# Moving the load of w4 behind two chunks of transposes, and the waits for the outputs to GpSimd

## The chip, the cores and the metric

The kernel runs on one core of a Trainium2 chip. The metric is the device time of one execution in microseconds; the time of a kernel is the median of its runs. A profile is one execution with the hardware profiler on. It gives times relative to the start of the program's span.

## What is computed

A gated mix of two blocks over one sequence of S = 2048 tokens with D = 640 channels, all in bf16. Block A is linear attention with 32 heads of 20; block B mixes tokens by shifts and ends in an MLP with F = 1728. Both read the same x.

```python
def reference(A_x, A_wqkv, A_wo, B_x, B_w1, B_w2, B_w3, B_w4, gate_w):
    ...                      # _A_ref: phi(q) (phi(k)^T v) / (phi(q) . sum phi(k)), then @ wo
    def _B_ref(x, w1, w2, w3, w4):
        h = _gelu(_layernorm(x, axis=-1) @ w1)
        ...                  # hs: four column groups of h, shifted by +1, -1, +2, -2 tokens
        hs = jnp.concatenate([g0, g1, g2, g3], axis=-1) @ w2
        x1 = x + hs
        h2 = _gelu(_layernorm(x1, axis=-1) @ w3) @ w4
        return x1 + h2
    x = A_x
    g = _sigmoid((x * gate_w).sum(-1, keepdims=True))
    a = _A_ref(x, A_wqkv, A_wo)
    b = _B_ref(x, B_w1, B_w2, B_w3, B_w4)
    return g * a + (1 - g) * b
```

## The kernel before

The tokens are cut into 16 tiles of 128 (t, u = 0 to 15) and four chunks of 512 (c = 0 to 3). The kernel works in stages that overlap: q and k for all tiles; the products of k with x, from which the attention's small matrix is made (item "kvt" multiplies it with the v weights, "lt", "m" and "mq" with wo; "ms" stores 40 rows of it to device memory and "mt" loads them back into M_sb); the first normalization (items "n1", "t1"), w1 with gelu, w2; the second normalization ("n2", "t2"), w3 with gelu into h2T, and w4. The attention tiles ("a") multiply the normalized q, transposed into pqnT (items "qs", "qn", "qt"), with M_sb. The last VectorE step of a tile (line 645) adds what w4 gave, and out_tiles stores the result from x_tok.

Engines: TensorE multiplies. ScalarE does exp, gelu and copies out of PSUM. VectorE does sums, scaling and residual adds. GpSimd normalizes (normalize writes one of four xn slots, line 628), computes the statistics, and scales x_tok into abx ahead of an attention tile. SyncE's queue issues nearly all DMAs: loads, stores and the transposes of xn into xnT (t_xn, four semaphores in turn, "trn0" to "trn3"), of pq_tok into pqnT (qt_tile) and of tlT into tl. The lines 285 and 289 of the helper dma are the transposes and the plain DMAs; line 318 is a wait that stands as an instruction of its own; line 321 is the closing barrier, and line 1404 holds the opening one.

The order of each engine's instructions is fixed when the kernel is built. Every step is an item of a stream with dependencies. The planner (_Items.run) keeps its own clock for every engine and issues, again and again, the item that could start first in that clock; items whose entry has duration 0 go ahead of matmul items, and among equals the longest remaining path decides. An item's dependencies count as done when its last instruction or DMA ends in the planner's clock. On the chip only the order in each engine's queue and the semaphores count: the helper _Sched keeps, for each address range, who wrote and read it, and adds the waits that are needed.

The loads of w3 and w4 are two items of the stream "MISC":

```python
    def w3_load():
        dma_in(w3[:, :, 0:F], B_w3.rearrange("(k p) f -> p k f", p=128), "w3")

    def w4_load():
        dma_in(w4[:, 0:KFF, :], B_w4[0:128 * KFF, :].rearrange("(k p) f -> p k f", p=128), "w4a")
        dma_in(w4[0:64, KFF, :], B_w4[128 * KFF:F, :], "w4b")
        dma_in(w4[64:128, KFF, :], B_w4[128 * KFF:F, :], "w4c")
```

KFF is 13: F is 13 blocks of 128 and one of 64, and the last 64 rows of w4 are loaded twice, for the groups that work with half of TensorE's rows (w3_half at line 1120, w4_enter at lines 1208 and 1213). The w4 tensor lies in memory that the first half of the kernel uses for wq, Er, wv and the first tiles of pk_tok. Items that depend on "w4load" are the attention tiles "a" (a planner's dependency only; they do not read w4) and the item of the second w3_half with the first w4_enter, which reads it.

At the end of the program, emit appends waits for the last DMA on each output semaphore, the last output first, and then the barrier. In the barrier each engine executes a DRAIN and reports; GpSimd collects the reports and releases all engines. The last tile's output leaves in two stores, 512 columns from ScalarE's queue and 128 from SyncE's.

Of the kernel before, what the change touches and what calls it, by code (L numbers as in the profile page):

```python
# [15 lines left out]
NT = S // 128  # L16
# [35 lines left out]
class _Sched:  # L52
# [247 lines left out]
    def emit(self):  # L300
        nc = self.nc
        with ExitStack() as es:
            sems = {}
            for e in ("pe", "act", "dve", "pool"):
                sems["c:" + e] = es.enter_context(nc.semaphore("cnt_" + e))
            for k in self.dma_cnt:
                sems["d:" + k] = es.enter_context(nc.semaphore("dma_" + k))
            seen = {w for p in self.prog.values() for (waits, _fn, _sem) in p for w in waits}
            last = {k: i for i, k in enumerate(self.out_order)}
            left = [k for k in self.dma_cnt if k not in last and ("d:" + k, 16 * self.dma_cnt[k]) not in seen]  # L310
            for k in sorted(last, key=last.get, reverse=True) + left:
                self.prog["sp"].append(([("d:" + k, 16 * self.dma_cnt[k])], None, None))
            engs = {"pe": nc.tensor, "act": nc.scalar, "dve": nc.vector, "pool": nc.gpsimd, "sp": nc.sync}

            for name, e in engs.items():
                for (waits, fn, sem) in self.prog[name]:
                    for (sk, val) in waits:
                        e.wait_ge(sems[sk], val)
                    if fn is not None:
                        fn(e).then_inc(sems[sem], 16 if sem.startswith("d:") else 1)  # L320
            nc.all_engine_barrier()
# [95 lines left out]
def _build(nc, A_x, A_wqkv, A_wo, B_w1, B_w2, B_w3, B_w4, gate_w, out, dbg=None, stop=None):  # L417
# [336 lines left out]
    IT = _Items()  # L754
# [521 lines left out]
    for c in range(NCH):  # L1276
        for j in range(KD):
            deps = [(("t1", u), 0.9) for u in range(4 * c, 4 * c + 4)] if j == 0 else []
# [6 lines left out]
    for t in range(NT):  # L1285
        c = t // 4
        deps = [(("w1", c, KD - 1), GEL)]
# [8 lines left out]
    for u in range(NT):  # L1296
        deps = [(("s2", u // 4), 3.2 + 0.9 * (u % 4))]
# [4 lines left out]
        IT.add("N2", ("n2", u), 0.0, lambda u=u: normalize(2, u, st2), deps)  # L1302
        IT.add("T2", ("t2", u), 0.0, lambda u=u: t_xn(2, u), deps=[(("n2", u), 1.1)])
    IT.add("MISC", ("w3load",), 0.0, w3_load, deps=[(("k", NT - 1), 0.0), (("t1", NT - 1), 0.0)])
    IT.add("MISC", ("w4load",), 0.0, w4_load, deps=[(("kvt",), 0.0), (("t1", NT - 1), 0.0), (("z", NT - 1), 1.5)])
    for c in range(NCH):
        for j in range(KFF):
            deps = []
# [4 lines left out]
            if j == 0:  # L1313
                deps = deps0 + [(("t2", u), 0.9) for u in range(4 * c, 4 * c + 4)]
# [11 lines left out]
    for t in range(NT):  # L1326
        deps = [(("zb",), 1.0), (("qr", max(t // 4, 1)), 2.0)]
# [14 lines left out]
    for t in range(NT):  # L1342
        c = t // 4
        deps = [(("qt", t), 3.0), (("w4load",), 0.0), (("mq",), 1.0), (("mt",), 2.5)]
# [38 lines left out]
def bass_gated_mix__linear_attn_block__mixer_s_mlp__prompt_kernel(  # L1383
    nc, A_x, A_wqkv, A_wo, B_x, B_w1, B_w2, B_w3, B_w4, gate_w, out
):
    assert tuple(A_x.shape) == (1, S, D) and tuple(out.shape) == (1, S, D)
    assert tuple(A_wqkv.shape) == (D, 3 * D) and tuple(A_wo.shape) == (D, D)
    assert tuple(B_w1.shape) == (D, D) and tuple(B_w2.shape) == (D, D)
    assert tuple(B_w3.shape) == (D, F) and tuple(B_w4.shape) == (F, D) and tuple(gate_w.shape) == (D,)
    _build(nc, A_x, A_wqkv, A_wo, B_w1, B_w2, B_w3, B_w4, gate_w, out)  # L1390
# [28 lines left out]
```

## Time and profile before

| | |
|---|---|
| median of 3 runs | 260.21 us (259.76 to 260.26) |
| profiled execution, its own time | 260.06 us |
| its span | 258.3 us, granted clock 1.00 |
| busy share of the span | TensorE 99%, VectorE 61%, ScalarE 43%, GpSimd 37% |
| DMA moved | 26.78 MB, mean 104 GB/s |

The profile's names: PE is TensorE's matmuls, PEld its weight loads, DVE is VectorE, ACT ScalarE, POOL GpSimd, SP SyncE; a q behind the name means the engine's sequencer, which waits, branches and issues DMAs. A row of groups names line, engine, operation, output<-inputs and count. In rows of one line or tile the three numbers after the count are the shortest, median and longest duration in ns, then come the first and last start in us. In rows of stretches each engine's busy time is followed by its number of instructions; the last three numbers are TensorE's granted clock, the mean busy share of the 16 DMA engines and the GB/s moved. The span does not hold all of the time: 260.06 - 258.3 = 1.76 us lie outside it.

### The profile page before, as it was taken

Reading aid. Unit: us, or ns where it says so; the run is one execution under the profiler, and the core shown is the slowest. Engines: PE = TensorE matmul, PEld = TensorE weight load, DVE = VectorE, ACT = ScalarE, POOL = GpSimd, SP = SyncE. Lnnn points to the kernel's source line nnn. Section 1 sums busy time; section 2 is a strip of 40 time slices with the busy share of each in tenths; the row PEclk is TensorE's granted clock in tenths of the full one; section 3 lists DMA queues with packets and bytes.
Section 4 is the critical chain, followed back from the end, with each engine's and each line's share of the span. In section 5 each row is a group of like instructions: output and inputs, shape, how many; then the busy total and the mean of one; then the engine's idle time right before and its main releaser. Section 6 shows DMA issues by size and latency. Waiting matters only on the chain.

```text
span 258.3 us, 3824 instructions
## 1 busy us (share of the span) xinstructions
PE 254.8 (99%) x1427; PEld 122.7 (47%) x1427; DVE 158.2 (61%) x293; ACT 110.9 (43%) x229; POOL 96.8 (37%) x154
## 2 busy tenths in 40 slices
PE   7999999999999999999999999999999999999996
PEld 3555555544444554554444444444444444444443
DVE  2597877899954699989995302999022530134076
ACT  1496777751355857684874240005500045200100
POOL 8014996869934119659681210111020120021000
DMA  6857997826527699483668512114200140000224
GB/s 194 263 101 235 139 141 193 231 55 119 102 49 105 124 392 305 82 101 65 127 124 117 102 20 23 25 25 130 42 3 0 20 124 0 0 0 1 43 84 139
DMA packets 58644, 26.78 MB, mean 104 GB/s; under 512 B 49966, under 2 KB 57215, under 8 KB 58626
## 3 DMA queue, kind: packets, MB, share of 16 engines
q1 hardware_dynamic: 57122, 22.92, 42.5%
q0 software_dynamic: 1168, 3.28, 5.4%
q10 hardware_dynamic: 336, 0.35, 0.4%
q8 instruction: 11, 0.18, 0.3%
q14 instruction: 7, 0.06, 0.1%
HBM read 12.09 MB, written 2.67 MB: 57 GB/s over the span
## 4 chain that ended last, share of the span: by engine, by line
PE 97%; DMA 1%; DVE 0%; issue 0%
PE ps L606 61%; PE ps L1233 22%; PE ps L812 7%; PE ps L893 2%; PE ps L792 1%; DMA x_tok<-in_A_x_dram 1%; PE ps L1120 1%; PE ps L1208 1%; PE ps L617 1%; PE ps L914 1%; PE ps L894 0%; PE ps L984 0%; PE ps L793 0%; PE ps L1213 0%; PE ps L1017 0%; DVE xT L671 0%
## 5 line engine op out<-in xcount | busy, mean ns | idle before, releaser
L606 PE MATMUL ps<-xnT,w 128*128 128x512 bf16 x360 | 81.3, 379 | 0.0
L606 PEld LDWEIGHTS ps<-xnT,w 128*128 128x128 bf16 x360 | 34.6, 98 | 39.3
L645 DVE SCALAR_TENSOR_TENSOR x_tok<-ps,stg,abx 128x512 bf16<-128x512 f32 (+2 forms) x17 | 12.2, 718 | 58.5 <-PE ps L1233 58.4
L1233 PE MATMUL ps<-w,h2T 128*128 128x512 bf16 (+2 forms) x221 | 47.2, 366 | 0.0
L628 POOL TENSOR_SCALAR abx<-x_tok,stg 128x512 f32<-128x512 bf16 x16 | 12.0, 753 | 88.2 <-DVE x_tok L645 70.1
L628 POOL TENSOR_SCALAR xn<-x_tok,st 128x640 bf16<-128x640 bf16 x32 | 38.6, 1215 | 8.6 <-DMA xnT<-xn 8.2
L662 ACT ACTIVATE h2T<-ps 128x512 bf16<-128x512 f32 x52 | 29.9, 599 | 22.7 <-PE ps L606 22.6
L1233 PEld LDWEIGHTS ps<-w,h2T 128*128 128x128 bf16 x221 | 21.2, 98 | 24.1
L662 ACT ACTIVATE tlT<-ps 128x512 bf16<-128x512 f32 x8 | 4.8, 597 | 64.1 <-PE ps L606 41.9
L662 ACT ACTIVATE Er<-ps 128x640 bf16<-128x640 f32 (+1 forms) x35 | 22.9, 658 | 17.8 <-PE ps L606 9.7
L661 ACT ACTIVATE junk<-x_tok 128x640 bf16<-128x640 bf16 x32 | 23.6, 737 | 4.7 <-DVE x_tok L643 4.2
L662 ACT ACTIVATE hsT<-ps 128x512 bf16<-128x512 f32 (+1 forms) x32 | 18.9, 593 | 14.2 <-PE ps L606 13.8
L606 PE MATMUL ps<-w,hsT 128*128 128x512 bf16 (+1 forms) x160 | 24.0, 299 | 0.0
L606 PE MATMUL ps<-wkg,xT 128*128 128x512 bf16 (+1 forms) x150 | 22.6, 299 | 0.0
L606 PE MATMUL ps<-M_sb,pqnT 128*128 128x512 bf16 x80 | 19.7, 379 | 0.0
L606 PEld LDWEIGHTS ps<-w,hsT 128*128 128x128 bf16 x160 | 13.4, 98 | 12.5
L645 DVE SCALAR_TENSOR_TENSOR abx<-ps,stg,abx 128x512 f32<-128x512 f32 x16 | 12.0, 750 | 10.7 <-PE ps L606 7.2
L606 PEld LDWEIGHTS ps<-wkg,xT 128*128 128x128 bf16 x150 | 12.6, 97 | 11.7
L643 DVE SCALAR_TENSOR_TENSOR x_tok<-ps,x_tok 128x640 bf16<-128x640 f32 x16 | 13.1, 821 | 7.6 <-PE ps L606 6.9
L812 PE MATMUL ps<-pk_tok,x_tok 128*128 128x512 bf16 x80 | 17.8, 379 | 0.0
L636 DVE TENSOR_TENSOR qprod<-qprod,pk_tok 128x640 f32<-128x640 f32 x13 | 16.3, 1252 | 0.5
L628 DVE TENSOR_SCALAR Er<-Er 128x640 bf16<-128x640 bf16 (+1 forms) x35 | 11.6, 332 | 7.6 <-ACT Er L662 6.8
(85 smaller groups left out, 282.9 us busy)
## 6 DMA issues: line engine op xcount, KB each, us to landing
w<-in_B_w_dram SPq DMA_DIRECT2D x1, 2160.0 KB, 9.5
w<-in_B_w_dram SPq DMA_DIRECT2D x1, 2080.0 KB, 15.0
x_tok<-in_A_x_dram SPq DMA_DIRECT2D x3, 640.0 KB, 5.6
out_dram<-x_tok SPq DMA_DIRECT2D x3, 640.0 KB, 3.5
w<-in_B_w_dram POOLq DMA_DIRECT2D x8, 160.0 KB, 6.2
wkg<-in_A_wqkv_dram SPq DMA_DIRECT2D x5, 160.0 KB, 3.9
wv<-in_A_wqkv_dram POOLq DMA_DIRECT2D x1, 800.0 KB, 5.6
x_tok<-in_A_x_dram SPq DMA_DIRECT2D x4, 160.0 KB, 3.2
```

What stands on the lines that cost most here:

```text
L606: ins = e.matmul(out_ap, l, r, start=(i == 0), stop=(i == n - 1))
L617: ins = e.transpose(o, s_, ident[:])
L628: return engf(lambda e: e.tensor_scalar(out_ap, in_ap, s1, s2, op0, op1), rd, [out_ap], cost=cost)
L636: return engf(lambda e: e.tensor_tensor(out_ap, a, b_, op), [a, b_], [out_ap], cost=cost)
L643: return dve(lambda e: e.scalar_tensor_tensor(out_ap, in0, scalar, in1, op0, op1, accum_out=accum), rd, [out_ap, accum], cost=cost + 70.0)
L645: return dve(lambda e: e.scalar_tensor_tensor(out_ap, in0, scalar, in1, op0, op1), rd, [out_ap], cost=cost)
L661: return act(lambda e: e.activation(out_ap, in_ap, func, bias=bias, scale=scale, accum_out=accum), rd, wr, cost=cost)
L662: return act(lambda e: e.activation(out_ap, in_ap, func, bias=bias, scale=scale), rd, wr, cost=cost)
L792: e.matmul(ps[:, b, :], l, x_tok[:, t, 0:512], start=(t == 0), stop=(t == NT - 1))
L812: ins = e.matmul(ps[:, b, :], l, r, start=(t0 + q_ == 0), stop=(t0 + q_ == NT - 1))
L893: e.matmul(ps[:, b, 0:512], l, w[:, k, 0:512], start=(k == 0), stop=(k == KD - 1))
L1233: ins = e.matmul(o, l, r, start=False, stop=(i == KFF - 1), skip_group_check=shared)
```

## The change

Two edits. The waits for the outputs, with those for DMAs that nothing else waited for, are appended to GpSimd's program instead of SyncE's. And the item "w4load" gets other dependencies: instead of the last tile of the first normalization's transposes ("t1", 15) and the last addition of z ("z", 15), it now depends on the store of the 40 rows ("ms") and on the eighth transpose of the second normalization ("t2", 7). The dependency on "kvt" stays. The item keeps its place in its stream, behind "w3load".

```diff
@@ -309,7 +309,7 @@
             for k in sorted(last, key=last.get, reverse=True) + left:
-                self.prog["sp"].append(([("d:" + k, 16 * self.dma_cnt[k])], None, None))
+                self.prog["pool"].append(([("d:" + k, 16 * self.dma_cnt[k])], None, None))
@@ -1302,7 +1302,7 @@
     IT.add("MISC", ("w3load",), 0.0, w3_load, deps=[(("k", NT - 1), 0.0), (("t1", NT - 1), 0.0)])
-    IT.add("MISC", ("w4load",), 0.0, w4_load, deps=[(("kvt",), 0.0), (("t1", NT - 1), 0.0), (("z", NT - 1), 1.5)])
+    IT.add("MISC", ("w4load",), 0.0, w4_load, deps=[(("kvt",), 0.0), (("ms",), 0.0), (("t2", 7), 0.0)])
```

## The prediction

> **What bounds the kernel now.** I read the page first: engine totals, then the chain that ended last in order of time.
>
> ```profile
> span 258.3 us, 3824 instructions
> ...
> PE 254.8 (99%) x1427; PEld 122.7 (47%) x1427; DVE 158.2 (61%) x293; ACT 110.9 (43%) x229; POOL 96.8 (37%) x154
> ```
>
> TensorE is busy for 254.8 of 258.3 us, and nearly every piece of the chain is its own. A busy share of 99% can still hide matmuls that start late, so I take pieces of the chain in order of time (start, length, what, how many).
>
> ```profile
> 127.91 22.77 PE ps L606 x105
> 150.68 2.28 PE ps L1120 x20
> ...
> 205.62 16.19 PE ps L606 x75
> ...
> 239.18 16.99 PE ps L1233 x91
> 256.17 0.03 issue
> 256.19 0.35 DVE x_tok L645
> ```
>
> Between 127.91 and 150.68 there are 105 matmuls at 22.77 / 105 = 0.217 us each; in a late stretch 75 of the same kind take 16.19 / 75 = 0.216 us each. The first stretch lies right behind the place to which the load is moved, and it is full without a gap: 105 x 0.001 us is all that could be won in it. The chain ends with TensorE at 256.17 and a last VectorE step at 256.19 to 256.54. What is left, 256.54 to 258.3, is the last store and the closing barrier. So the change has two places where it can act: the stretch from 88 to 151 us, by making TensorE wait, and the last 1.8 us.
>
> **The load of w4, where it goes away.** It now stands in SyncE's queue behind w3's load. Issues (size, microseconds to landing), then the same issues with their own durations (shortest/median/longest ns, first and last start), then stretches with TensorE's busy time ahead of the other engines', and at the end the DMA share and GB/s.
>
> ```profile
> w<-in_B_w_dram SPq DMA_DIRECT2D x1, 2160.0 KB, 9.5
> w<-in_B_w_dram SPq DMA_DIRECT2D x1, 2080.0 KB, 15.0
> ```
> ```profile
> L289 SPq DMA_DIRECT2D w<-in_B_w_dram x4: 523/936/5852, 88.1 to 95.2; - x4
> ```
> ```profile
> 88.00:95.00 7.00, 7.00 (x46) 3.60 (x44) 5.95 (x15) 4.26 (x9) 0.20 (x1) 1.00 0.92 304
> 95.00:100.00 5.00, 5.00 (x32) 2.59 (x31) 4.90 (x11) 4.61 (x11) 3.57 (x7) 1.00 1.05 370
> ...
> sum 63.00, PE 63.00 PEld 30.61 DVE 49.79 ACT 39.76 POOL 32.97; mean PE 3.94 PEld 1.91 DVE 3.11 ACT 2.48 POOL 2.06
> ```
>
> w3 and w4 together keep the DMA engines full (shares 0.92 and 1.05), and one of the four issues holds SyncE for 5.85 us. Yet the last row sums sixteen stretches from 88 to 151 us, and TensorE is busy in 63.00 of 63.00. Taking w4 out of 88 to 104 us makes transposes behind it land earlier, but nothing on the path was late: gain 0.
>
> **Where it goes to.** SyncE's queue there, by the timeline of its issues (start, time until the group's last issue ended):
>
> ```profile
> 100.80 13.82 SPq L285 DMA_TRANSPOSE xnT<-xn  x8
> 114.66 0.56 SPq L289 DMA_DIRECT2D m_rows<-Mt  x1
> 118.91 5.29 SPq L285 DMA_TRANSPOSE xnT<-xn  x4
> 124.30 8.26 SPq L285 DMA_TRANSPOSE pqnT<-pq_tok  x6
> 132.66 5.76 SPq L285 DMA_TRANSPOSE xnT<-xn  x4
> ```
>
> The first eight xnT transposes are the two chunks that the load is to follow; its other new dependency, the store of m_rows, stands at 114.66. So three issues (one of 2080 KB, two of 80 KB) move past eight transposes and one store, and come to stand at 115.22, in front of the ninth transpose. That one waits for GpSimd's xn until 118.91, so SyncE has 118.91 - 115.22 = 3.69 us free.
>
> Cost of the three issues: at best 3 x 0.52 = 1.6 us, which the 3.69 hide. At worst the stall of 5.85 comes along, with one issue of the shortest and one of the median length: 0.52 + 5.85 + 0.94 = 7.3 us, and the ninth transpose goes out 7.3 - 3.69 = 3.6 us late. I take the lower end, because the issue of 5.85 us stood behind w3's 2160 KB, which is no longer in front of it. The data is 2240 KB, 2.29 MB; at the 304 to 370 GB/s of the rows above that is 6.2 to 7.5 us, so it lands at about 123, and at the worst, with the old 15.0 us, at 131.
>
> Who waits for what stands behind it:
>
> ```profile
> L606 PE MATMUL ps<-M_sb,pqnT x80: 379/379/379, 138.6 to 234.2; 128*128 128x512 bf16 x80
> ```
> ```profile
> L1213 PE MATMUL ps<-h2h,w x8: 269/274/280, 152.9 to 238.9; 64*128 64x256 bf16 x8
> ```
> ```profile
> L285 SPq DMA_TRANSPOSE xnT<-xn x16: 1200/1276/1795, 100.8 to 136.6; - x16
> ...
> DMA to landing us min/median/max: 2.6/2.7/4.7
> ```
> ```profile
> 129.10 4.66 POOL L628 TENSOR_SCALAR xn<-x_tok,st 128x640 bf16<-128x640 bf16 x4
> ```
>
> w4 itself is first read at 152.9: at least 22 us after the latest landing. The first pqnT transpose goes out at 124.3 and lands 2.7 later, at 127.0; TensorE first reads pqnT at 138.6, a margin of 11.6. The last xnT transpose starts at 136.6 and, with the longest landing of 4.7, is there by 141.3; it is read by the half-width groups at 150.68, a margin of 9.4. GpSimd's xn slots of the fourth chunk wait for the third chunk's transposes; the first of those lands at 118.91 + 2.7 = 121.6 and GpSimd starts at 129.10, a margin of 7.5. Even the worst delay, 3.6 us of queue and a landing longer by 4.7 - 2.6 = 2.1, is 5.7 and under all of these. The cover is TensorE's queue of w3 groups (the 105 matmuls); without it each microsecond of delay would be one of time. In the planner the attention tiles wait for the load too; the first of them, the reader of pqnT at 138.6, comes after the latest landing of 131, so TensorE's order has no reason to change. Moved load: 0.
>
> **The waits at the end.** The last store, SyncE's waits for the outputs, and the closing barrier (L321), beside the opening barrier (L1404) and GpSimd's last work:
>
> ```profile
> L289 SPq DMA_DIRECT2D out_dram<-x_tok x1: 345/345/345, 256.6 to 256.6; - x1
> ...
> DMA to landing us min/median/max: 1.5/1.5/1.5
> ```
> ```profile
> L318 SPq EVENT_SEMAPHORE  x2: 137/457/777, 257.1 to 257.9; - x2
> ```
> ```profile
> L321 POOLq EVENT_SEMAPHORE  x2: 17/17/17, 258.2 to 258.2; - x2
> L321 POOLq DRAIN  x1: 2797/2797/2797, 233.2 to 233.2; - x1
> ...
> L321 ACTq DRAIN  x1: 146/146/146, 256.5 to 256.5; - x1
> L321 SPq DRAIN  x1: 13/13/13, 258.1 to 258.1; - x1
> ```
> ```profile
> L1404 POOLq DRAIN  x1: 169/169/169, 0.4 to 0.4; - x1
> ```
> ```profile
> 233.26 0.69 POOL L628 TENSOR_SCALAR abx<-x_tok,stg 128x512 f32<-128x512 bf16 x1 [1.55 <-DVE x_tok L645]
> ```
>
> The store lands at 256.6 + 1.5 = 258.1; SyncE's wait ends there, its DRAIN takes 13 ns, then GpSimd collects (two records at 258.2) and releases everybody by 258.3. With the waits on GpSimd, SyncE drains right after its last issue, at about 256.9, beside the store. GpSimd now wakes at 258.1 itself, and one hop between engines falls away; but its DRAIN, which today starts at 233.2 beside 22 us of other work, moves behind the last landing and onto the path. Queued behind the wait on GpSimd are this DRAIN and the two records that release the barrier; all engines wait for those.
>
> So the term is: GpSimd's DRAIN, less SyncE's 13 ns and less a hop that is at most the 0.1 to 0.2 us between 258.1 and 258.2 to 258.3. Its price is not shown for an engine that has been idle. Lower end: it takes no time at all, and with the hop the sum is -0.1. Upper end: the one DRAIN of the closing barrier on GpSimd took 2.80 us, of which 233.26 + 0.69 = 233.95 minus 233.2, 0.75, were its last operation, and 2.05 came after. I take 0.1, from the rows in which a DRAIN had nothing of its engine in front of it or only a few small writes: SyncE's 13, ScalarE's 146 (right behind a DMA issue), GpSimd's own 169 in the opening barrier. In the changed kernel GpSimd has had no operation for 24 us when its DRAIN starts, which is nearer to these than to the one issued together with a 0.69 us operation. The Trainium skill, page "VectorE: DVE Perf Modes", section "The DRAIN you can't avoid", says that the boilerplate DRAINs take a constant 12 ns or so on all five engines. By that rule the sum would be 260.2; the 13 ns of SyncE agree, the 2797 and 169 ns of GpSimd do not, so I don't rest on it.
>
> **The sum.** The profiled execution took 260.06 us: 258.3 of span and 1.76 around it. 0 for the load, +0.1 for the end: 260.16. The median of the three runs, 260.21, lies 0.15 above the profiled one, so the forecast is **260.3 us**.
>
> **The rivals.** *GpSimd's DRAIN is long whatever stood before it* (slower). If the 2.05 us after 233.95 are what the DRAIN does itself, they now stand between the last landing and the release: 260.21 + 2.05 = 262.3. For it: it is the only DRAIN on GpSimd after real work, and nothing in the timeline of GpSimd explains the 2.05. Against: 169 ns in the opening barrier. It decides from a DRAIN of about 0.6 us on. The Trainium skill, page "GPSIMD Engine Reference", section "Instruction dispatch", says that the first call of a freshly loaded routine pays about 6 us for loading its code; by that the end could be 266, but no run here shows such a load. Chance 0.28; another 0.07 for a DRAIN between 0.6 and 1.5 us, 260.8 to 261.7.
>
> *The moved load starves TensorE* (slower). If SyncE is held not for 7.3 but for the whole 15.0 us of the old landing, the ninth transpose leaves at 130.2 instead of 118.9, 11.3 late; the last xnT lands at 141.3 + 11.3 = 152.6, the half-width groups start 1.9 late, and the time is 262.1. It decides from a hold of 9.4 + 3.7 = 13.1 us on, more than twice the longest issue seen. Chance 0.05.
>
> *The end gets shorter by more than the hop* (faster). SyncE is through 258.1 - 256.9 = 1.2 us earlier; if its share of the 1.76 us outside the span could start then, up to 1.2 is won: 259.0. Against: the release at 258.3 holds all engines, SyncE too. Chance 0.05.
>
> *The order does not change as said.* Should the load come to stand behind the third chunk's transposes as well, it lands some 9 us later, still over 10 us ahead of 152.9: again about 260.3. Chance 0.05.
>
> **How the numbers follow.** The forecast has 0.50. A measurement of this kernel can tell about 0.2%, 0.52 us, from no change; within that lie the forecast and the last rival, 0.55. Slower: 0.28 + 0.07 + 0.05 = 0.40. Faster: 0.05. The likeliest case alone spans 260.0 to 260.6 (DRAIN from 13 to 169 ns, the hop, and the 0.5 us by which the runs differ, 259.76 to 260.26). The whole range reaches down to the lowest run, 259.8, and up to the long DRAIN with 0.1 for its hop, 262.4; left out are the gain and the starved case's and DRAIN's far ends, under 0.15.
>
> **What would show it.** Right: TensorE's last piece ends within 0.1 us of 256.17; the three w issues stand at 115 us and take under 3.7 us; GpSimd's DRAIN starts at about 258.1 and takes under 0.2 us; SyncE's DRAIN stands at 256.9. Wrong: a DRAIN of 1 us or more on GpSimd behind the last landing; a TensorE gap at 138.6 or 150.7 that is released by a transpose; a ninth xnT transpose after 130.

## The result and the profile after

The change made the kernel slower: 261.88 us (261.71 to 262.4, six runs) against 260.06 us (259.76 to 260.26, six runs), a ratio of 1.0075 with a 95% interval of 1.0062 to 1.0088, or 1.8 us. The profiled execution took 261.86 us with a span of 260.1. The time is inside the stated range, but it is that of the first rival, which had 0.28, and not that of the forecast, 260.3.

The page of the changed kernel, and the end of its chain in order of time (start, length, what, how many):

```profile
span 260.1 us, 3797 instructions
...
PE 253.2 (97%) x1400; PEld 122.5 (47%) x1427; DVE 158.4 (61%) x293; ACT 110.9 (43%) x229; POOL 96.8 (37%) x154
```
```profile
238.99 2.91 PE ps L1233 x13
241.95 10.74 PE ps L1233 x49
252.69 0.05 issue
252.74 3.23 PE ps L1233 x27
256.00 0.35 DVE x_tok L645
```

A lower busy share of TensorE looks like lost time in it, but the page says 1400 matmuls beside 1427 weight loads: 27 records are missing from this trace. In the last stretch 13 + 49 + 27 = 89 matmuls stand where 91 stood before, and there are two gaps of 0.05 us, at 241.90 and 252.69; the stretch as a whole is not longer (239.18 to 256.17 before, 238.99 to 255.97 here). So such a piece of "issue" is the place of a missing record, not lost time. TensorE itself was not later than before: the last VectorE step begins at 256.00, where it began at 256.19. All of the loss, and 0.19 us more, lies behind it. The closing barrier, and the waits ahead of it, now on GpSimd:

```profile
L321 POOLq EVENT_SEMAPHORE  x2: 17/17/17, 259.9 to 260.0; - x2
...
L321 ACTq DRAIN  x1: 147/147/147, 256.3 to 256.3; - x1
L321 SPq DRAIN  x1: 136/136/136, 256.8 to 256.8; - x1
L321 POOLq DRAIN  x1: 2028/2028/2028, 257.9 to 257.9; - x1
```
```profile
L318 POOLq EVENT_SEMAPHORE  x2: 17/372/727, 256.9 to 257.0; - x2
```

GpSimd's DRAIN starts at 257.9, when the last store has landed (issued at 256.4, 1.5 us to landing), takes 2.03 us although GpSimd has had no operation since 234 us, and its two barrier records follow at 259.9 and 260.0 instead of 258.2. The account: -0.19 (VectorE's last step, earlier) + 2.03 (GpSimd's DRAIN) - 0.01 (SyncE's DRAIN of 13 ns, gone from the path) = 1.83; the span grew by 1.8.

The other edit did what it says. SyncE's issues around the load (start, time until the group's last issue ended), then the durations of all w issues and of the transposes with their landings:

```profile
114.45 0.56 SPq L289 DMA_DIRECT2D m_rows<-Mt  x1
115.06 2.64 SPq L289 DMA_DIRECT2D w<-in_B_w_dram  x3
118.72 8.62 SPq L285 DMA_TRANSPOSE xnT<-xn  x4
127.44 8.32 SPq L285 DMA_TRANSPOSE pqnT<-pq_tok  x6
135.86 6.09 SPq L285 DMA_TRANSPOSE xnT<-xn  x4
```
```profile
L289 SPq DMA_DIRECT2D w<-in_B_w_dram x4: 583/592/1371, 88.1 to 117.1; - x4
```
```profile
L285 SPq DMA_TRANSPOSE xnT<-xn x16: 1200/1276/2864, 100.6 to 140.7; - x16
...
DMA to landing us min/median/max: 2.6/2.7/8.2
```

The issue of 5.85 us is gone; the longest of a w load is now 1.37. The hold has not vanished with it, it has moved to those who come next: the four transposes behind the load take 8.62 us to issue instead of 5.29, and the first of them lands 8.2 us after its issue. The load itself lands later after its issue than its size over the rates of before gave, 6.2 to 7.5 us:

```profile
w<-in_B_w_dram SPq DMA_DIRECT2D x1, 2080.0 KB, 10.8
```

### The profile page after: what moved, and what is told of

Read it like the earlier page. It is cut to its first block, busy times and chain, and to the rows that moved or that the text cites. A ratio compares the mean times of both kernels' runs of the same rounds, so it can differ in the third digit from the quotient of the medians.

```text
span 260.1 us, 3797 instructions
## 1 busy us (share of the span) xinstructions
PE 253.2 (97%) x1400; PEld 122.5 (47%) x1427; DVE 158.4 (61%) x293; ACT 110.9 (43%) x229; POOL 96.8 (37%) x154
## 3 DMA queue, kind: packets, MB, share of 16 engines
q0 software_dynamic: 1168, 3.28, 5.2%
## 4 chain that ended last, share of the span: by engine, by line
PE 80%; DVE 12%; DMA 2%; ACT 2%; issue 1%; SPq 1%; DVEq 0%
PE ps L606 52%; PE ps L1233 22%; DVE qprod L636 7%; PE ps L893 2%; DVE x_tok L643 2%; DMA x_tok<-in_A_x_dram 1%; ACT h2T L662 1%; DMA xnT<-xn 1%; PE ps L792 1%; PE ps L1120 1%; DVE pq_tok L1147 1%; PE ps L1208 1%; DVE dnr L1130 1%; ACT junk L661 1%; DVE zsum L636 1%
## 5 line engine op out<-in xcount | busy, mean ns | idle before, releaser
L606 PE MATMUL ps<-xnT,w 128*128 128x512 bf16 x351 | 80.0, 379 | 0.6 <-DMA xnT<-xn 0.2
L1233 PE MATMUL ps<-w,h2T 128*128 128x512 bf16 (+2 forms) x215 | 46.4, 366 | 0.3
L606 PE MATMUL ps<-w,hsT 128*128 128x128 bf16 (+1 forms) x159 | 23.8, 298 | 0.1
L628 DVE TENSOR_SCALAR Er<-Er 128x640 bf16<-128x640 bf16 (+1 forms) x35 | 11.6, 332 | 7.6 <-ACT Er L662 6.8
## 6 DMA issues: line engine op xcount, KB each, us to landing
w<-in_B_w_dram SPq DMA_DIRECT2D x1, 2080.0 KB, 10.8
```

The source lines that it names most:

```text
L606: ins = e.matmul(out_ap, l, r, start=(i == 0), stop=(i == n - 1))
L628: return engf(lambda e: e.tensor_scalar(out_ap, in_ap, s1, s2, op0, op1), rd, [out_ap], cost=cost)
L1233: ins = e.matmul(o, l, r, start=False, stop=(i == KFF - 1), skip_group_check=shared)
```

## The experiments

Theory A was the long DRAIN of GpSimd, now behind the last landing. Its rivals were a cost of the moved load, and a cost of waiting on any engine but SyncE. Behind that stood the question what makes this DRAIN long.

**The waits alone** (e1), the load at its old place:

```diff
-                self.prog["sp"].append(([("d:" + k, 16 * self.dma_cnt[k])], None, None))
+                self.prog["pool"].append(([("d:" + k, 16 * self.dma_cnt[k])], None, None))
```

> Only the waits go to GpSimd; the load of w4 keeps its old place. Theory A (GpSimd's DRAIN, now behind the last landing, is the whole loss): a DRAIN of about 2.0 us at 258 us and 1.8 to 2.0 us more than the kernel before, about 261.9. Theory B (the moved load costs part of it, through the third chunk's transposes, which are issued up to 3 us later): less than 1.5 us more. Theory C (nothing but noise between runs): no change.

Measured: 262.16 us against 260.11, ratio 1.0079 (1.0064 to 1.0094). The closing barrier's row on GpSimd:

```profile
L321 POOLq DRAIN  x1: 2028/2028/2028, 258.2 to 258.2; - x1
```

The waits alone bring the whole loss, with the same 2028 ns as in the full change.

**The load alone** (e2), the waits on SyncE:

```diff
-... w4_load, deps=[(("kvt",), 0.0), (("t1", NT - 1), 0.0), (("z", NT - 1), 1.5)])
+... w4_load, deps=[(("kvt",), 0.0), (("ms",), 0.0), (("t2", 7), 0.0)])
```

> Only the load moves; the waits stay on SyncE. Theory A: within 0.2 us of the kernel before, 260.1, although the four transposes behind the load take some 3 us longer to issue. Theory B: 0.5 to 1.8 us more, with a TensorE gap at one of the readers (138.6 or 150.7 us).

Measured: 260.25 against 260.11, ratio 1.0005 (0.9995 to 1.0014). The load neither costs nor gains what can be told apart; theory B falls.

**The waits on ScalarE** (e3), the load moved:

```diff
-                self.prog["pool"].append(([("d:" + k, 16 * self.dma_cnt[k])], None, None))
+                self.prog["act"].append(([("d:" + k, 16 * self.dma_cnt[k])], None, None))
```

> The changed kernel with the waits on ScalarE instead of GpSimd. Theory A (it is GpSimd's DRAIN and not the waiting): ScalarE's DRAIN, 0.15 us or less, stands behind the last landing, and the time is within 0.2 us of the kernel before, about 260.1. Rival (any engine but SyncE pays for the waits): about 262.

Measured: 260.02 against 260.11, ratio 0.9998 (0.9988 to 1.0008). The DRAINs of GpSimd and ScalarE in the closing barrier:

```profile
L321 POOLq DRAIN  x1: 2800/2800/2800, 232.8 to 232.8; - x1
...
L321 ACTq DRAIN  x1: 8/8/8, 257.7 to 257.7; - x1
```

Behind the last landing ScalarE's DRAIN takes 8 ns, and GpSimd's is back at 232.8, beside TensorE's work. It is not the waiting; it is whose DRAIN stands behind it.

**No DMA issued by GpSimd** (e4): in load_w1, load_w2 and load_wvo of the changed kernel each

```diff
-            sch.dma("pool", w1[:, :, 128 * g_:128 * (g_ + 1)],
+            sch.dma("sp", w1[:, :, 128 * g_:128 * (g_ + 1)],
...
```

> The changed kernel, with the 24 loads that GpSimd issued (w1, w2, wv, wo) issued by SyncE instead; the waits stay on GpSimd. Theory S (the DRAIN is long because GpSimd issued DMAs earlier in the program): its DRAIN falls under 0.2 us, and the time to about 260.0, if SyncE's queue bears the loads. Theory T (the DRAIN is long by itself, or by GpSimd's arithmetic before it): still 2.0 us at the end, about 261.9.

Measured: 260.10 against 260.11, ratio 0.9999 (0.9989 to 1.0008).

```profile
L321 POOLq DRAIN  x1: 41/41/41, 258.4 to 258.4; - x1
```

The waits are still on GpSimd, and the DRAIN behind the landing takes 41 ns. What made it long are DMAs that GpSimd issued before 50 us, 200 us earlier. GpSimd's arithmetic is the same here (130 instructions instead of 154: the 24 DMA issues are what is gone), so theory T falls.

**One more DRAIN, ahead of the waits** (e5) and **behind them** (e6), both in the changed kernel (the edit of e5; in e6 the new line stands behind the loop):

```diff
+            self.prog["pool"].append(([], lambda e: e.drain(), None))
             for k in sorted(last, key=last.get, reverse=True) + left:
...
```

> The changed kernel with one more DRAIN in GpSimd's program, ahead of the waits for the outputs, so that it runs at 233 us beside TensorE's work. Theory E (every DRAIN of GpSimd pays, because GpSimd has issued DMAs at some time): the added one and the barrier's both take about 2.0 us, and the time stays at 261.9. Theory F (only the first DRAIN after the DMAs pays, say for tidying up their descriptors): the barrier's falls under 0.2 us, and the time to about 260.0.

> The changed kernel with one more DRAIN in GpSimd's program behind the waits for the outputs, directly ahead of the barrier's. Theory E: two DRAINs of 2.0 us one after the other, 263.9. Theory F: 2.0 and under 0.2, 262.0.

Measured: e5 260.16 against 260.08, ratio 1.0004 (0.9994 to 1.0014); e6 262.19, ratio 1.0084 (1.0069 to 1.0099). In e5 the added DRAIN is line 311 and the barrier line 324; in e6 line 313 and 324.

```profile
L311 POOLq DRAIN  x1: 2797/2797/2797, 232.8 to 232.8; - x1
```
```profile
L324 POOLq EVENT_SEMAPHORE  x2: 17/17/17, 257.7 to 257.8; - x2
L324 POOLq DRAIN  x1: 47/47/47, 257.6 to 257.6; - x1
```
```profile
L313 POOLq DRAIN  x1: 2028/2028/2028, 258.1 to 258.1; - x1
```
```profile
L324 POOLq DRAIN  x1: 40/40/40, 260.1 to 260.1; - x1
```

Only the first DRAIN pays. Moved to 232.8 it costs nothing, and the barrier's own is short even with the waits on GpSimd. Theory E falls.

**DRAINs at several places** (e7), in the kernel before. The lines are 692 (behind the first memset), 748 and 749 (behind the setup), 712 (ahead of w1's loads), 849 and 850 (ahead of the second normalization); 323 is the barrier. One execution took 260.19 us; it was run for the lengths of the DRAINs.

> The kernel before with six more DRAINs on GpSimd: one after its first memset, two after its setup, one ahead of the loads of w1 (its first DMAs), two ahead of the second normalization. No time is wanted, only their lengths. Theory E: the first four, ahead of any DMA of GpSimd, take under 0.2 us beyond the work in front of them; the last two, 50 us after its last DMA has landed, about 2.0 us each. Theory F: the second of the last two is short. A third theory, that the routines which the affine selects load at 1 to 2 us make a DRAIN slow: the ones after the setup already take 2 us.

```profile
L748 POOLq DRAIN  x1: 4511/4511/4511, 2.9 to 2.9; - x1
```
```profile
L749 POOLq DRAIN  x1: 41/41/41, 7.4 to 7.4; - x1
```
```profile
L712 POOLq DRAIN  x1: 449/449/449, 22.0 to 22.0; - x1
```
```profile
98.59 0.20 POOL L630 TENSOR_SCALAR st<-st 128x4 f32<-128x4 f32 x1
```
```profile
L849 POOLq DRAIN  x1: 2295/2295/2295, 98.5 to 98.5; - x1
```
```profile
L850 POOLq DRAIN  x1: 47/47/47, 100.9 to 100.9; - x1
```
```profile
L323 POOLq DRAIN  x1: 814/814/814, 233.3 to 233.3; - x1
```

The one of line 692, behind a single memset, took 181 ns. The 4511 ns at 2.9 are the setup's memsets in front of it, the last of which ends at 4.00 + 3.30 = 7.30; the next one, behind the same setup and its affine selects, takes 41 ns, so the third theory falls. The 449 ns at 22.0 are the last operation too, which ends at 22.38. All of these stand ahead of GpSimd's first DMA. At 98.5 the operation in front ends at 98.59 + 0.20 = 98.79, and the DRAIN at 100.8, 2.0 us later; the second takes 47 ns. The barrier's DRAIN, 2797 ns before, is down to 814, its last operation and little more. So the price is paid once for the DMAs issued since the last DRAIN, 50 us after the last of them or 200, as theory F said.

**One load on GpSimd's queue** (e8: wv) and **eight** (e9: w1), the others on SyncE's, in the changed kernel:

> The changed kernel with one load (wv) on GpSimd's queue instead of 24, the others on SyncE's. If the DRAIN costs the same as soon as GpSimd has issued any DMA: 2.0 us at the end. If its cost goes with the number of DMAs: between the 41 ns measured without any and 41 + 1990 / 24 = 124 ns.

> The changed kernel with the eight loads of w1 on GpSimd's queue (0.82 MB in all) and the other sixteen on SyncE's. A price for each DMA, from 0 DMAs (41 ns), 1 (147) and 24 (2028): 41 + 8 x 83 to 8 x 106, so a DRAIN of 0.70 to 0.89 us. A price by bytes, from the 3.28 MB that GpSimd moves in the changed kernel: 0.82 / 3.28 of 1.99 us, 0.54 us.

```profile
L321 POOLq DRAIN  x1: 147/147/147, 257.7 to 257.7; - x1
```
```profile
L321 POOLq DRAIN  x1: 727/727/727, 258.3 to 258.3; - x1
```

| DMAs that GpSimd issued | 0 | 1 | 8 | 24 |
|---|---|---|---|---|
| moved by them, MB | 0 | 0.82 | 0.82 | 3.28 |
| DMA packets of their queue | 0 | 176 | 384 | 1168 |
| DRAIN behind the last landing, ns | 41 | 147 | 727 | 2028 |

From one DMA to eight (727 - 147) / 7 = 83 ns each, from eight to 24 (2028 - 727) / 16 = 81 each; the first takes 106. One load and eight loads that move the same bytes differ by 0.58 us, so it goes by the number and not by the bytes. A price by packets fits worse: 0.6 ns for each of the first 176, (727 - 147) / 208 = 2.8 ns for each of the next 208, (2028 - 727) / 784 = 1.7 ns for each of the rest. The first expectation for e8, a constant price, and the price by bytes, fall; the 124 ns by proportion were 23 short, and for e9 the price for each DMA, 0.70 to 0.89 us, held. The lengths for 0, 1 and 8 DMAs are from one trace each, the 2028 ns stood in three (the changed kernel, e1, e6). One execution took 259.81 us for e8 and 260.99 for e9.

**The load later still** (e10), the waits on SyncE: `("t2", 15)` in the place of `("t2", 7)`.

> The waits on SyncE, and the load of w4 behind the transposes of all four chunks of the second normalization, some 24 us later than in the change. If TensorE's queue still covers it (it should land by about 150 us, and is read at 152.9): within 0.2 us of the kernel before. If the cover ends here: a TensorE gap at 152.9 and up to 5 us more.

Measured: 260.29 against 260.15, ratio 1.0002 (0.9992 to 1.0013). SyncE's issues, and the landings of the four w loads:

```profile
132.36 6.12 SPq L285 DMA_TRANSPOSE xnT<-xn  x4
138.53 2.20 SPq L289 DMA_DIRECT2D w<-in_B_w_dram  x3
140.77 10.57 SPq L285 DMA_TRANSPOSE pqnT<-pq_tok  x6
```
```profile
DMA to landing us min/median/max: 7.7/8.5/9.5
```

Even from 138.5 the data is there by about 148, ahead of its first reader at 153. The hold moves with the load: the six pqnT transposes behind it take 10.57 us to issue, where they took 7.88 before. At none of the three places tried, at 88, 115 and 138 us, does the load cost anything that can be told apart. Where that ends was not tried.

No version ran below the kernel before by more than the interval: e3 and e5, the changed kernel with the long DRAIN out of the way, are at 0.9998 and 1.0004.

## Why the prediction was right, and where it was wrong

By the range, the time was forecast; by the mechanism, it was not. The likeliest case ended at 260.6, below the lowest run, 261.71; the range holds the time because it was drawn up to the first rival. Of the signs that were named, the first for "wrong" came: a DRAIN of 1 us or more on GpSimd behind the last landing.

**What bounds the kernel**: right. Every kernel here has the same 1427 weight loads of TensorE in the same order, and the last VectorE step of the changed one starts within 0.2 us of before; only the end moved. TensorE's last piece ended 0.2 us earlier than before, at 255.97, a little more than the 0.1 us that the sign allowed.

**The load taken away**: gain 0, right (e2). **The load put in**: cost 0, right, by the cover that was named. The issues took 2.64 us and fitted the 3.69 us that were free, as said. The reason given was too kind: that the hold is gone without w3's load in front. The issue of 5.85 us in the trace before was that of 80 KB of w4 at 89.3 us, and it stood behind w4's own 2080 KB as well as behind w3. In the changed kernel the hold moved to the transposes behind the load, 3.3 us more for the four, within the bound of 3.6; the landing of 8.2 us lay above the 4.7 used as the longest, and the load landed 10.8 us after its issue, not 7.5. The margins of 7.5 to 11.6 us took all of it.

**The waits**: wrong, and this is the step that failed: "I take 0.1". The term was named and its place on the path was right; its size was 2.03 us, the upper end of the bounds to within 0.02. I chose between 13 ns and 2.05 us by what stood in front of the DRAIN in time, an idle engine or a running operation. What decides is what GpSimd had issued earlier: the opening barrier's 169 ns, which I took for a near row, was taken ahead of GpSimd's first DMA, and the 2.80 us behind its last. Of the rows compared, only the 2.80 us came from an engine in the same state, a GpSimd with DMAs issued since its last DRAIN. The hop that was to fall away gave nothing that can be measured (e5, 1.0004).

**The rivals**: the first was right in its place and nearly in its price, 262.3 against 261.88, but its mechanism, "long whatever stood before it", was not: a second DRAIN takes 40 to 47 ns, and without DMAs the first does as well. Starvation did not come, at either new place of the load; the load stood where it was forecast, and the end did not get shorter with the long DRAIN out of the way (e3, e5). The sentence of the Trainium skill, page "VectorE: DVE Perf Modes", section "The DRAIN you can't avoid", that such DRAINs take about 12 ns on all five engines holds here for SyncE (13 ns) and ScalarE (8) when they have just waited, not for these two right behind a DMA issue of their own (136 and 147 in the changed kernel), and not for GpSimd (41 without DMAs, 2028 with 24). The code load of about 6 us that the Trainium skill, page "GPSIMD Engine Reference", section "Instruction dispatch", states played no part: with the same arithmetic and no DMAs the DRAIN took 41 ns.

## What to carry to other kernels

Before an engine is given the last wait of a program, ask what its DRAIN still has to do; on GpSimd that was about 82 ns for each DMA that it had issued, and the place for that was beside work, not behind the last landing. If GpSimd must wait at the end, one DRAIN ahead of the waits takes the price off the path (e5). When a term lies between rows that are more than ten times apart, look for what differs in the history of the engine between them, not only for what is in front of the instruction.

## What the runs showed that was not expected

- A DRAIN on GpSimd pays 81 to 106 ns for each DMA that GpSimd issued since its last DRAIN, 50 or 200 us after they were issued (41, 147, 727 and 2028 ns for 0, 1, 8 and 24). What the engine does in that time no run showed.
- SyncE's queue passes a hold on: with w3's load no longer in front, the issues of w4 fell from up to 5.85 us to at most 1.37, and a transpose behind them took 2.86 us to issue instead of 1.28 and up to 8.2 to land.
